# Four batches instead of two take the 32-bit path for the early rows' exponents, and 14 unread products are placed before the second batch's first turn

## The chip, the cores and the metric

The program runs on one core of a Trainium2 chip. The metric is the device time of one execution in microseconds; the figure compared is the median of several executions. A core has a matrix engine (TensorE, PE in the profile, with its weight loads as PEld), a vector engine (VectorE, DVE), an activation engine (ScalarE, ACT), GpSimd (POOL) and SyncE (SP), whose queue issues most of the transfers.

## The reference, cut to what matters

The input has 4 batches of 576 positions and 8 heads of width 64. Three parts follow one another: attention under a mask of blocks of 64, then two feed-forward parts, the second behind a two-dimensional Fourier transform.

```python
scores = scale * np.matmul(q, k.transpose(0, 1, 3, 2))
mask = block_i >= block_j                    # blocks of 64 positions
scores = np.where(mask, scores, -1000000000.0)
scores = scores - np.max(scores, axis=-1, keepdims=True)
attn = np.exp(scores)
attn = attn / (np.sum(attn, axis=-1, keepdims=True) + 1e-09)
attn_out = np.matmul(attn, v)
...
xn = (x - mu) / np.sqrt(var + 1e-06) * g_ln
x = x + np.maximum(xn @ w_ch1, 0.0) @ w_ch2  # 512 -> 2048 -> 512
...
u = x + np.real(np.fft.fft(np.fft.fft(x, axis=1), axis=2))
out = u + np.maximum(norm(u) @ w2_ch1, 0.0) @ w2_ch2
```

## The kernel before

The rows of a batch are cut in three: E is its first 256 positions (the early rows), F another 256, and L holds the 32 or so positions that are left over, of all four batches together. The kernel first computes the attention of the early rows of all batches (E0 to E3), and meanwhile loads the first feed-forward's weights and splits them into a high and a low 16-bit half. As soon as E0 is there, the first feed-forward begins with it (`gemm1`, L632, 8 steps of 24 products per row group; then `gemm2`), and the attention of the remaining rows runs between its products, from `a_switch` on. Everything behind that is the second half and is not touched by the change.

The early rows of a batch are worked off in four pairs of heads, written below as (batch, pair). For each pair: `e_s` computes the scores with 32-bit products (L957) and adds the mask (L917); `e_exp` takes the row maxima on VectorE (L971, L972) and the exponents on ScalarE (L975, four instructions); `e_norm_p` brings the exponents into the transposed layout that the product with V needs; `e_pv` multiplies them with V; `e_x` divides by the row sums on VectorE (L1039, L1042, L1045). There are two ways through the two steps in the middle, and the tuple `ET` says which batches take which:

- The 32-bit way (batches 0 and 1 before the change): `e_turn` transposes the six blocks of 128x128 exponents on TensorE (L986) and ScalarE copies them out of PSUM (L990). `e_pv` first issues `NBUSY` = 4 unread products of 240 columns into the unused part of its PSUM bank (L874), and then six 32-bit products of 65 columns (L1011; each stands as two entries in a trace).
- The 16-bit way (batches 2 and 3): ScalarE and VectorE split the exponents into two halves (`p_split`, L923 and L924), a transposing DMA on SP's queue turns them (`p_turn`, L930), and `e_pv` issues 18 16-bit products (L895). V is scaled and split too (`e_v`, L904 to L908).

V of a 32-bit batch lies in a tile `rv`, of which there are `RVE` = 1 buffers; its four loads (L858) wait for the products of the batch before.

Instructions are written down by `merge`, a planner that interleaves streams by costs, and their order on each engine is then set by a scheduler with priorities. Two things fix a place by hand: `in_order(f)` puts what f issues behind the last TensorE instruction written so far, and `A["busy"]` is a PSUM tile for the unread products in front of batch 0's first turn. Tiles of PSUM for feed-forward products come from `g_tile`, a ring of two buffers, which also gives the tiles `xt` of the normalised rows' turns (`ln_turn`, L587, read by ScalarE at L591 and VectorE at L592).

Of the kernel before, what the change touches and what calls it, by code (L numbers as in the profile page):

```python
# [25 lines left out]
G1P = 20  # L26
G2P = 1
ST = 2
RVE = 1
RAWE = 3  # L30
AP = 20
DW = (3, 5)
# [10 lines left out]
NB = 1  # L43
P_D = 0
EL = 1
ET = (0, 1)
QZ = 3
KB = 3
PSC = 2.0 ** 14
# [6 lines left out]
X0B = 2  # L56
TURN = ((1, ("E", 0)), (1, ("E", 1)))
NBUSY = 4
G1E = 1
LNA = 2  # L60
ESP = 20
# [38 lines left out]
def fused_kernel(ctx: ExitStack, tc: tile.TileContext, io: dict):  # L100
# [14 lines left out]
    def g_tile(shape, name):  # L115


        pool = psg
        if "x" in psn:
            pool = psn["x"] if psn["n"] % (GB + GX) >= GB else psg  # L120
            psn["n"] += 1
        return pool.tile(shape, F32, tag="g", name=name)
# [492 lines left out]
    def gemm1(ffn, c, mp):  # L615
# [21 lines left out]
        h = hT[ffn, c][mp // 2][:, 2 * (mp % 2):2 * (mp % 2) + 2]  # L637
        prio(g1_out, G1E if ffn == 1 and c in (("E", 0), ("E", 1)) else G1P)(ps, h)

# [170 lines left out]
    A = {}  # L810
    ap_ = {}

    def prio(f, n=None):
        def g(*a):
            if (n or AP) <= 0:
                return f(*a)
            with tc.high_priority(n or AP):
                return f(*a)
        return g
# [6 lines left out]
    def a_tile(shape, dt, tag, name):  # L826
        return ap_["p"].tile(shape, dt, tag=tag, bufs=ap_["b"][tag], name=name)
# [25 lines left out]
    def e_load(b):  # L853
        if b in ET:
            r = a_tile([128, NPAIR * 4, 66], F32, "rv", f"rv{b}")
            nc.gpsimd.memset(r[:, :, 64:65], 1.0)
            for p in range(NPAIR):
                (nc.sync if b else nc.scalar).dma_start(  # L858
                    out=r[:, 4 * p:4 * p + 4, 0:64],
                    in_=io["vt"][b, p][:, 0:2, :].rearrange("k c (h d) -> k (c h) d", h=2),  # L860
                )
            A["ev", b] = r
            return
        r = a_tile([128, NPAIR, 256], F32, "rv", f"rv{b}")
        nc.sync.dma_start(
            out=r.rearrange("k p (c d) -> k p c d", c=2),
            in_=io["vt"][b].rearrange("p k c d -> k p c d")[:, :, 0:2, :],
        )
        A["rv", b] = r

    def busy(n, out):

        for _ in range(n):
            nc.tensor.matmul(  # L874
                out=out, lhsT=late[:, 0, :],
                rhs=late.rearrange("p k n -> p (k n)")[:, 0:out.shape[-1]], start=True, stop=True,
            )

    def e_raw(b, p):

        r = a_tile([128, 2, 256], F32, "rz", f"rz{b}{p}")
        nc.sync.dma_start(out=r[:, 0], in_=io["qt"][b, p][:, S:S + 256])
        nc.sync.dma_start(out=r[:, 1], in_=io["kt"][b, p][:, 0:256])
        A["raw", b, p] = r
# [36 lines left out]
    def p_split(e, P, n):  # L921

        nc.scalar.activation(out=P[:, 0, 0:n], in_=e, func=AF.Copy, scale=PSC)  # L923
        nc.vector.scalar_tensor_tensor(  # L924
            out=P[:, 1, 0:n], in0=e, scalar=PSC, in1=P[:, 0, 0:n], op0=ALU.mult, op1=ALU.subtract
        )

    def p_turn(P, blocks):
        PT = a_tile([128, blocks, 128], F16, "PT", "PT")
        nc.sync.dma_start_transpose(out=PT, in_=P.rearrange("p a k -> p (a k)"))  # L930
        return PT
# [13 lines left out]
    def e_s(b, p):  # L945
        with ExitStack() as order:
            if "f" in ff_last:
                order.enter_context(tc.issue_after(ff_last["f"]))
            prio(e_products, ESP)(b, p)
        ff_last["e"] = last_pe()  # L950
# [14 lines left out]
    def e_exp(b, p):  # L965
        st = A.pop(("st", b, p))
        e = a_tile([128, 2, 384], F32, "e", "e")
        q = sm.tile([128, 2, 2, 2], F32, tag="eq", bufs=3, name="eq")
        mx, nb = q[:, 0], q[:, 1]
        for t, (o, w) in enumerate(EO):  # L970
            nc.vector.tensor_reduce(out=mx[:, t], in_=st[:, :, o:o + w], axis=AX.X, op=ALU.max)  # L971
        nc.vector.tensor_scalar(out=nb, in0=mx, scalar1=-0.125, scalar2=None, op0=ALU.mult)  # L972
        for t, (o, w) in enumerate(EO):
            for h in range(2):
                nc.scalar.activation(  # L975
                    out=e[:, h, o:o + w], in_=st[:, h, o:o + w], func=AF.Exp, scale=0.125,
                    bias=nb[:, t, h:h + 1],
                )
        A["e", b, p] = (e, st) if b in ET else e

# [12 lines left out]
    def e_norm_p(b, p):  # L993
        if b in ET:
            return prio(e_turn, ESP)(b, p)
        e = A.pop(("e", b, p))
        P = a_tile([128, 2, 768], F16, "P", "P")
        p_split(e.rearrange("p h k -> p (h k)"), P, 768)
        A["PT", b, p] = p_turn(P, 12)

    @(lambda f: prio(f, EPP))
    def e_pv(b, p):
        if b in ET:
            v, e = A["ev", b], A.pop(("PT", b, p))
            bank = pso.tile([128, 512], F32, tag="o", name="pv")
            busy(NBUSY, bank[:, 272:512])
            ps = bank[:, 0:260].rearrange("q (t h d) -> q t h d", t=2, h=2)
            for t in range(2):
                for h in range(2):
                    for c in range(t + 1):  # L1010
                        nc.tensor.matmul(  # L1011
                            out=ps[:, t, h], lhsT=e[:, h, 128 * (t + c):128 * (t + c) + 128],
                            rhs=v[:, 4 * p + 2 * c + h, 0:65], start=(c == 0), stop=(c == t),
                        )
            A["pv", b, p] = (ps, None)
            return
        vh, vl, s = A["ev", b]
        PT = A.pop(("PT", b, p)).rearrange("k (a h c) q -> k a h c q", a=2, h=2)
        ps = pso.tile([128, 2, 2, 65], F32, tag="o", name="pv")
        for t in range(2):  # L1020
            for h in range(2):
                mm = []
                for c in range(t + 1):
                    n = 4 * p + 2 * c + h
                    for a, v, w in ((0, vh, 65), (0, vl, 64), (1, vh, 65)):
                        mm.append((PT[:, a, h, t + c], v[:, n], w))
                pv(ps[:, t, h], mm)
        A["pv", b, p] = (ps, s)
# [21 lines left out]
    def e_items(b):  # L1050
        def head():
            e_raw(b, 0)
            e_load(b)

        def front(p):
            if p + 1 < NPAIR and b not in ET:
                e_raw(b, p + 1)
            e_s(b, p)
            e_exp(b, p)
            e_norm_p(b, p)  # L1060

        def back(p):
            e_pv(b, p)
            e_x(b, p)

        def two():
            for p in range(2):
                e_s(b, p)
                e_exp(b, p)
            in_order(lambda: (busy(NBUSY, A["busy"][:, 0:384]), e_norm_p(b, 0)) if b == 0 else e_norm_p(b, 0))  # L1070

        if b in ET:
            return [
                (0.0, lambda: [e_raw(b, p) for p in range(3 if b == 0 else 2)], (), None),
                (4.0, lambda: (two(), e_load(b)), (), None),
                (2.0, lambda: (e_raw(b, 2) if b else None, e_norm_p(b, 1)), (), None),
                (3.0, lambda: (e_raw(b, 3), front(2), back(0)), (), None),
                (3.0, lambda: (front(3), back(1)), (), None),
                (1.0, lambda: back(2), (), None),
                (1.0, lambda: back(3), (), ("X1", ("E", b))),  # L1080
            ]

        out = [(0.0, head, (), None), (3.0, lambda: front(0), (), None)]
        out.append((1.0, lambda: e_v(b), (), None))
        for p in range(1, NPAIR):
            out.append((3.0, lambda p=p: (front(p), back(p - EL) if p >= EL else None), (), None))
        for p in range(NPAIR - EL, NPAIR):
            out.append((1.0, lambda p=p: back(p), (), ("X1", ("E", b)) if p == NPAIR - 1 else None))
        return out
# [201 lines left out]
    def last_pe():  # L1291
        return next(
            i for i in reversed(nc.cur_bb.bb.instructions) if i.engine == mybir.EngineType.PE
        )

    def in_order(f):

        with tc.issue_after(last_pe()):
            f()
# [258 lines left out]
    if True:  # L1558
# [31 lines left out]
        ap_["first"] = True  # L1590
        a_open(dict(stage=ST, rv=RVE, rz=RAWE, warm=1, vh=2, vl=2, e=E1B[0], P=E1B[1], PT=E1B[2], xnT0=1, xn0=X0B, unit=1))
        warm = a_tile([128, 1], F32, "warm", "warm")
# [215 lines left out]
```

## Time and profile before

| what | value |
|---|---|
| runs (3) | 980.14, 982.59, 985.02 us; median 982.59 us |
| the profiled execution's own time | 979.0 us |
| its span, first to last instruction | 977.2 us |
| PE busy | 927.8 us, 95% of the span |
| DVE busy | 682.4 us, 70% |
| ACT busy | 491.1 us, 50% |
| mean granted TensorE clock | 0.983 |

The profiled execution is one run of its own, taken by the hardware profiler; it is 3.6 us shorter than the median of the three timed runs. Busy shares are means over stages with different limits, and matmuls are pipelined, so that a busy PE is not PE at its peak.

### The profile page before, as it was taken

The numbers are of one execution on the slowest core, as the hardware profiler recorded it, in microseconds if no ns is written. First come the engines' busy times: TensorE is split into PE (matmuls) and PEld (weight loads), VectorE is DVE, ScalarE is ACT, GpSimd is POOL, SyncE is SP. The second block draws the span as 40 slices with busy tenths as digits, with TensorE's granted clock in tenths as the row PEclk, the third lists the DMA queues.
The fourth block names the chain that finished last, engine by engine and source line by source line (L and its number), as shares of the span: only waits on it lengthen the run. The fifth ranks groups of instructions, "written<-read, shape, count | busy, mean of one in ns | idle before, by whom it ended". The sixth has DMA issues, their size and how long they took to land.

```text
span 977.2 us, 19373 instructions
## 1 busy us (share of the span) xinstructions
PE 927.8 (95%) x7694; PEld 690.0 (71%) x7694; DVE 682.4 (70%) x1716; ACT 491.1 (50%) x860; POOL 73.7 (8%) x183
## 2 busy tenths in 40 slices
PE   8888899997998999999999899999999999999998
PEld 5666644673664765757485767757688888888887
DVE  4887986666667575566599888689486676665754
ACT  5798835554554555437466654335144252352431
POOL 1000000002011020040012201100000000000000
PEclk9798999999999999999999999999999999999999
DMA  8657446667668667577308765102110210101100
GB/s 283 219 201 238 99 122 139 139 130 145 128 141 146 138 139 100 99 188 277 108 22 247 250 217 183 27 11 65 34 22 23 45 22 23 33 24 33 23 23 22
DMA packets 159178, 110.68 MB, mean 113 GB/s; under 512 B 134181, under 2 KB 141350, under 8 KB 157040
## 3 DMA queue, kind: packets, MB, share of 16 engines
q1 hardware_dynamic: 154640, 104.87, 41.6%
q0 software_dynamic: 2336, 4.06, 1.8%
q8 instruction: 60, 0.98, 0.4%
q10 hardware_dynamic: 2112, 0.52, 0.2%
q14 instruction: 30, 0.25, 0.1%
HBM read 63.93 MB, written 11.01 MB: 77 GB/s over the span
## 4 chain that ended last, share of the span: by engine, by line
PE 43%; DVE 7%; DMA 4%; ACT 3%; issue 1%; POOL 0%; SPq 0%; ACTq 0%; DVEq 0%; POOLq 0%
PE g L703 15%; PE s L753 13%; PE g L632 6%; PE g L684 4%; PE g L657 3%; DMA wr<-in_w 2%; DVE wq L345 1%; DVE ws L224 1%; ACT junk L245 1%; DVE hT L642 1%; PE pq L1499 1%; PE ya L1469 1%; DMA d<-ws 1%; ACT sign L223 1%; DMA xnT2('F', 0)_8023<-xs 1%
## 5 line engine op out<-in xcount | busy, mean ns | idle before, releaser
L632 PEld LDWEIGHTS <-wq 128*128 128x128 f16 x2112 | 205.9, 99 | 41.7 <-issue 14.1
L657 PE MATMUL g<-wq,hT 128*128 128x512 f16 x768 | 183.9, 383 | 2.6 <-ACT hT L641 1.6
L703 PEld LDWEIGHTS <-wq 128*128 128x128 f16 x1344 | 131.5, 98 | 15.4
L657 PEld LDWEIGHTS <-hT 128*128 128x128 f16 x768 | 74.6, 99 | 90.4 <-issue 5.5
L753 PEld LDWEIGHTS <-hs 128*128 128x128 f16 x1176 | 115.1, 98 | 13.3
L895 PE MATMUL pv<-vh,PT 128*128 128x65 f16 (+1 forms) x704 | 102.7, 203 | 19.6 <-DMA PT<-P 10.0
L720 ACT ACTIVATE hr<-g,tk 128x256 f32<-128x256 f32 x112 | 47.0, 470 | 143.5 <-PE g L703 143.5
L895 PEld LDWEIGHTS <-PT 128*128 128x128 f16 x1056 | 81.3, 101 | 33.7 <-issue 19.5
L924 DVE SCALAR_TENSOR_TENSOR P<-e,P 128x768 f16<-128x768 f32 (+2 forms) x56 | 54.6, 975 | 68.0 <-ACT P L923 67.9
L728 DVE TENSOR_TENSOR hr<-hr 128x128 f32<-128x128 f32 x224 | 65.4, 292 | 48.3 <-ACT hr L720 40.3
L1177 ACT ACTIVATE e<-st,aq 128x384 f32<-128x384 f32 (+2 forms) x80 | 48.9, 651 | 89.7 <-DVE aq L1174 77.0
L753 PE MATMUL s<-tT,hs 128*128 128x256 f16 x672 | 75.7, 273 | 0.0
L642 DVE SCALAR_TENSOR_TENSOR hT<-g,hT 128x512 f16<-128x512 f32 x88 | 59.7, 682 | 16.4 <-ACT hT L641 16.2
L641 ACT ACTIVATE hT<-g 128x512 f16<-128x512 f32 x88 | 51.3, 584 | 34.9 <-PE g L632 34.8
L684 PE MATMUL g<-wq,hT 128*128 128x512 f16 x288 | 63.9, 379 | 0.0
L895 PE MATMUL pv<-vl,PT 128*128 128x64 f16 (+1 forms) x352 | 62.5, 202 | 0.0
L735 DVE TENSOR_TENSOR hs<-hr,hs 128x896 f16<-128x896 f32 x56 | 60.7, 1084 | 0.5
L753 PE MATMUL s<-tB,hs 128*128 128x256 f16 x504 | 57.3, 273 | 0.0
L223 ACT ACTIVATE sign<-wr 128x512 f16<-128x512 bf16 (+1 forms) x48 | 46.5, 969 | 16.6 <-DMA wr<-in_w 12.9
L734 ACT ACTIVATE hs<-hr 128x896 f16<-128x896 f32 x56 | 53.1, 948 | 1.6 <-DVE hr L728 1.6
L224 DVE SCALAR_TENSOR_TENSOR ws<-wr,sign 128x512 int32<-128x512 int32 (+1 forms) x48 | 41.2, 864 | 17.3 <-ACT sign L223 16.6
L684 PEld LDWEIGHTS <-hT 128*128 128x128 f16 x288 | 28.0, 98 | 31.8
(432 smaller groups left out, 1504.7 us busy)
## 6 DMA issues: line engine op xcount, KB each, us to landing
wr<-in_w SPq DMA_DIRECT2D x16, 1023.5 KB, 6.2
wr<-in_w SPq DMA_DIRECT2D x32, 511.8 KB, 4.7
rawv<-in_vt SPq DMA_DIRECT2D x16, 320.0 KB, 3.2
k<-in_kt SPq DMA_DIRECT2D x16, 288.0 KB, 3.4
d<-ws SPq DMA_DIRECT2D x4, 1024.0 KB, 4.8
ws<-d SPq DMA_DIRECT2D x4, 1024.0 KB, 5.2
wt<-d SPq DMA_DIRECT2D x4, 1024.0 KB, 4.8
qz<-in_qt SPq DMA_DIRECT2D x32, 80.0 KB, 3.2
```

What stands on the lines that cost most here:

```text
L223: nc.scalar.activation(out=z[:, :, :, 1], in_=r.bitcast(BF16)[:, :, :, 2], func=AF.Copy)
L632: nc.tensor.matmul(out=ps[:, i, :], lhsT=w1(ffn, k, wh, m), rhs=xt[:, xh, k, :], start=(n == 0), stop=(n == 3 * KT - 1),)
L642: nc.vector.scalar_tensor_tensor(out=h[:, :, 1, :], in0=ps, scalar=0.0, in1=h[:, :, 0, :], op0=ALU.max, op1=ALU.subtract,)
L657: nc.tensor.matmul(out=ps, lhsT=h[f // 4][:, f % 4, hh, t * 128:(t + 1) * 128], rhs=w2(ffn, f, wh), start=(f == 0 and hh == 0 and wh == 0) ...
L684: nc.tensor.matmul(out=g2["b"][t], lhsT=h[f // 4][:, f % 4, hh, t * 128:(t + 1) * 128], rhs=w2(ffn, f, wh), start=(f == 0 and hh == 0 and ...
L703: nc.tensor.matmul(out=ps[:, q, :], lhsT=w1(2, k, wh, i + 8 * q), rhs=xt[:, xh, k, :], start=(n == 0), stop=(n == 3 * KT - 1),)
L728: done = nc.vector.tensor_tensor(out=r[:, o], in0=r[:, a], in1=r[:, b], op=op)
L734: nc.scalar.activation(out=h[:, 0], in_=r[:, 1:8], func=AF.Copy)
L735: nc.vector.tensor_tensor(out=h[:, 1], in0=r[:, 1:8], in1=h[:, 0], op=ALU.subtract)
L753: nc.tensor.matmul(out=ps, lhsT=h[:, hh, hb], rhs=T[nm][:, wh, i], start=(i == 0 and hh == 0 and wh == 0), stop=(i == 7 and hh == 1),)
L895: nc.tensor.matmul(out=out[..., 0:w], lhsT=l, rhs=v[..., 0:w], start=(n == 0), stop=(n == len(mm) - 1))
L924: nc.vector.scalar_tensor_tensor(out=P[:, 1, 0:n], in0=e, scalar=PSC, in1=P[:, 0, 0:n], op0=ALU.mult, op1=ALU.subtract)
```

## The change

Batches 2 and 3 move to the 32-bit way (`ET`), `rv` gets a second buffer (`RVE`), and 14 unread products of 384 columns are issued ahead of batch 1's first turn, into a new tile from the ring of `g_tile`. Below `e_items`, batches 2 and 3 now take the list of items of the 32-bit branch: two pairs' scores and exponents first, V's loads then, and a later start of the products with V.

```diff
-RVE = 1
+RVE = 2
...
-ET = (0, 1)
+ET = (0, 1, 2, 3)
...
+NBUSY1 = 14
...
-            in_order(lambda: (busy(NBUSY, A["busy"][:, 0:384]), e_norm_p(b, 0)) if b == 0 else e_norm_p(b, 0))
+            if b == 0:
+                in_order(lambda: busy(NBUSY, A["busy"][:, 0:384]))
+            elif b == 1:
+                in_order(lambda: busy(NBUSY1, g_tile([128, 512], "busy")[:, 0:384]))
+            in_order(lambda: e_norm_p(b, 0))
```

The scheduler's order moves with it. On TensorE, in front of E0's first feed-forward product, the kernel before has these rows (e_379 and e_397 are the exponents of pairs (1,0) and (1,1), xn0 are E0's normalised rows, rv1 is batch 1's V; a bracket names what the instruction waits for).

```order
L874 MATMUL pv_612<-late_83 128x240
L986 MATMUL st_370<-unit_117,e_379 128x128 [waits DVE_49,Activation_49]
L1011 MATMUL pv_520<-rv1_414,PT_412 128x65 [waits DMAHW6_49,Activation_49,Pool_49]
L986 MATMUL st_388<-unit_117,e_397 128x128 [waits DVE_49,Activation_49]
L874 MATMUL pv_663<-late_83 128x240 [waits PE_49]
L587 MATMUL xt_332<-unit_117,xn0_330 128x128 [waits DVE_49]
L587 MATMUL xt_341<-unit_117,xn0_339 128x128 [waits DVE_49]
L1011 MATMUL pv_612<-rv1_414,PT_453 128x65 [waits DMAHW7_49,Activation_49]
L632 MATMUL g1_464<-xnT0_329,wq110_360 128x256 [waits Activation_49]
```

With the change the same place reads as follows (all lines of the file move down by one; busy_406 is the new tile of the unread products).

```order
L875 MATMUL pv_627<-late_83 128x240
L987 MATMUL st_388<-unit_117,e_397 128x128 [waits DVE_49,Activation_49]
L588 MATMUL xt_332<-unit_117,xn0_330 128x128 [waits DVE_49]
L588 MATMUL xt_341<-unit_117,xn0_339 128x128 [waits DVE_49]
L875 MATMUL busy_406<-late_83 128x384 [waits DVE_49]
L987 MATMUL st_370<-unit_117,e_379 128x128 x6
L633 MATMUL g1_479<-xnT0_329,wq110_360 128x256 [waits DVE_49]
```

The turn of pair (1,1) now stands first, then E0's turns, then the 14 products, which wait for VectorE, then the turn of (1,0); both pairs' products with V (L1011) have moved behind E0's first feed-forward step.

On VectorE, in the chain of small steps that normalises E0, the kernel before has a pair's division in the middle, which waits for TensorE.

```order
L224 SCALAR_TENSOR_TENSOR ws_422<-wr_356,sign_119 128x1024
L552 TENSOR_TENSOR ln1('E', 0)_310<-ln1('E', 0)_310 128x2
L1039 TENSOR_SCALAR rr<-pv 128x4
L553 SCALAR_TENSOR_TENSOR ln1('E', 0)_310<-ln1('E', 0)_310 128x2
L1042 RECIPROCAL rr<-rr 128x4
```

With the change the chain stands there alone.

```order
L225 SCALAR_TENSOR_TENSOR ws_437<-wr_356,sign_119 128x1024
L553 TENSOR_TENSOR ln1('E', 0)_310<-ln1('E', 0)_310 128x2
L554 SCALAR_TENSOR_TENSOR ln1('E', 0)_310<-ln1('E', 0)_310 128x2
```

The division of (1,0) has moved behind the feed-forward's first step.

On TensorE, in batch 3, the kernel before places 18 products of 16 bits per pair between feed-forward products (here at pair (3,1); the last two rows repeat with the other blocks).

```order
L684 MATMUL g_1581<-wq_1544,hT 128x512
L895 LDWEIGHTS PT
L895 MATMUL pv<-vh_1385,PT 128x65
L895 LDWEIGHTS PT
L895 MATMUL pv<-vl_1386,PT 128x64
```

With the change each pair of batches 2 and 3 has a turn, placed inside a feed-forward step, and later four unread products and six products of 32 bits.

```order
L685 MATMUL g_1575<-wq_1497,hT 128x512
L987 MATMUL st<-unit,e 128x128 x6
L685 LDWEIGHTS hT
...
L685 MATMUL g_1576<-wq_1497,hT 128x512
L875 LDWEIGHTS late
L875 MATMUL pv<-late 128x240
...
L1012 MATMUL pv<-rv_1351,PT 128x65 x6
```

From the feed-forward's `gemm2` of E0 on, behind the last early pair, TensorE's order is the same in both kernels.

## Rows read from the trace of the kernel before

**Rows 1.** Busy time by stretch: from:to, length, engines (instructions), granted clock, DMA share, GB/s

```profile
core 0: us, PE busy (x) PEld busy (x) DVE busy (x) ACT busy (x) POOL busy (x), PEclk, DMA share, GB/s
30.24:44.54 14.30, 9.98 (x50) 8.70 (x50) 10.99 (x38) 9.92 (x18) 0.38 (x1) 0.64 0.70 218
44.54:78.85 34.31, 30.25 (x251) 24.00 (x250) 29.88 (x80) 30.02 (x44) 1.77 (x4) 0.95 0.55 189
78.85:97.47 18.62, 14.77 (x142) 11.87 (x138) 13.75 (x34) 15.45 (x27) 1.51 (x3) 0.91 0.98 304
97.47:146.06 48.59, 44.15 (x403) 27.79 (x403) 42.08 (x109) 29.90 (x48) 1.98 (x11) 1.00 0.49 109
```

**Rows 2.** PE's waits from 44.5 to 146 us: total, times, longest

```profile
PE pv L895 <- DMA PT<-P: 8.3, 6, 3.8
...
PE st L986 <- ACT e L975: 0.8, 2, 0.4
```

**Rows 3.** Instructions in time order before the first feed-forward: start, length, engine, line

```profile
33.04 1.54 PE L986 MATMUL st<-unit,e 128*128 128x128 f32 x6 [2.79 <-ACT e L975]
...
33.56 0.37 ACT L975 ACTIVATE e<-st,eq 128x128 f32<-128x128 f32 x1 [0.58 <-DVE eq L972]
...
38.35 0.16 DVE L1039 TENSOR_SCALAR rr<-pv 128x4 f32<-128x4 f32 x1 [2.96 <-PE pv L1011]
...
40.08 1.00 DVE L570 TENSOR_SCALAR xn<-XxE,ln1('E', 0)_310 128x512 f32<-128x512 f32 x2
...
40.68 1.97 PE L587 MATMUL xt<-unit,xn 128*128 128x128 f32 x8 [0.28 <-DVE xn L570]
...
43.21 1.28 DVE L592 TENSOR_TENSOR xnT<-xt,xnT 128x512 f16<-128x512 f32 x2
...
44.54 2.67 PE L632 MATMUL g<-xnT,wq 128*128 128x256 f16 x23 [0.31 <-DVE xnT L592]
```

**Rows 4.** Busy time of two stretches, columns as in rows 1

```profile
33.04:42.44 9.40, 8.17 (x36) 7.15 (x37) 6.09 (x26) 6.71 (x10) 0.38 (x1) 0.50 0.73 259
...
94.57:97.03 2.46, 2.46 (x26) 2.00 (x27) 1.19 (x4) 0.84 (x3) 0.00 (x0) 0.50 1.07 386
```

**Rows 5.** PE's 32-bit and unread products in time order, 2 to 60 us

```profile
2.51 1.76 PE L874 MATMUL busy<-late 128*128 128x384 bf16 x5
...
56.10 1.45 PE L1011 MATMUL pv<-rv,PT 128*128 128x65 f32 x12
...
57.39 0.57 PE L874 MATMUL pv<-late 128*128 128x240 bf16 x4
...
57.80 0.71 PE L632 MATMUL g<-xnT,wq 128*128 128x256 f16 x5
...
58.94 0.88 PE L986 MATMUL st<-unit,e 128*128 128x128 f32 x6 [0.44 <-ACT e L975]
...
59.66 1.04 PE L632 MATMUL g<-xnT,wq 128*128 128x256 f16 x8
```

**Rows 6.** One 16-bit pair in batch 2, PE alone, in time order

```profile
104.36 0.20 PE L895 MATMUL pv<-vh,PT 128*128 128x65 f16 x1 [1.21 <-DMA PT<-P]
...
104.92 1.25 PE L632 MATMUL g<-xnT1('E', 1)_848,wq 128*128 128x256 f16 x10
```

**Rows 7.** Around E1's turns, in time order

```profile
71.10 0.63 PE L587 MATMUL xt<-unit,xn 128*128 128x128 f32 x4 [1.79 <-DVE xn L570]
...
73.33 4.60 PE L632 MATMUL g<-xnT,wq 128*128 128x256 f16 x24 [0.60 <-DVE xnT1('E', 1)_848 L592]
```

**Rows 8.** Groups by line from 60 to 146 us: busy, mean ns, idle before

```profile
L924 DVE SCALAR_TENSOR_TENSOR P<-e,P 128x768 f16<-128x768 f32 x8 | 7.6, 949 | 0.0
...
L908 DVE SCALAR_TENSOR_TENSOR vl<-rv,pw,vh 128x1024 f16<-128x1024 f32 x2 | 2.6, 1277 | 0.0
```

**Rows 9.** The last early pair and the first score of the later attention

```profile
137.00 0.20 PE L895 MATMUL pv<-vh,PT 128*128 128x65 f16 x1 [1.01 <-DMA PT<-P]
...
146.06 0.92 PE L1153 MATMUL st<-k,qz 64*128 64x384 f32 x4
```

## Prediction

> **What bounds the kernel now.** I read the busy times by stretch first, to find where TensorE still has room. In the stretch up to the first feed-forward product it is busy 9.98 of 14.30 us at a granted clock of 0.64; from there to 78.85 us 30.25 of 34.31; then 14.77 of 18.62; and from 97.47 to 146.06 us, where batches 2 and 3 are mostly worked off, 44.15 of 48.59 [rows 1]. In the last of these ScalarE (29.90) has much room and VectorE (42.08) little more than TensorE. So TensorE is the engine to add work to last, and what can be won is its idle time and its half clock.
>
> The view of TensorE's waits says what that idle time is: 8.3 us in six waits for the transposing DMA, the longest 3.8; the exponents of a 32-bit pair cost it 0.8 us in two waits [rows 2]. The instructions in time order show the front: before 33.04 us TensorE has waited 2.79 us for the exponents of (1,0), and from there the clock stays at 0.50, that is 1.2 of 2.4 GHz, until 42.44 us although the engine is busy 8.17 of 9.40 us, with 32-bit turns, sums and a few unread products [rows 3, 4]. After the 3.8 us wait it is 0.50 again for 2.46 us [rows 4].
>
> From the attention's first score at 146.06 us on TensorE's order doesn't change. I take the time there as the handle: whatever that instruction is late or early, the end is too.
>
> **The change part by part.** The sum stands against the profiled execution's own 979.0 us.
>
> *A, the start of the first feed-forward (44.54 us before [rows 3]).* The order shows that the 14 products don't cover the wait for the second batch's exponents: the turn of (1,1) and E0's own turns stand ahead of them, and they wait for VectorE, because their tile is the ring buffer that E0's first turns leave. Walked through: TensorE is idle from 30.25 us (33.04 less 2.79) until the exponents of (1,1). Their first instruction starts at 33.56; without the copy of (1,0) between them, four of 0.37 at most end by 35.0. The turn at half clock takes 1.54: 36.5. VectorE's chain for E0 no longer waits 2.96 us for the pair's sum, nor does its division; so the normalised rows, at 40.08 to 41.08 before, come some 3.5 us earlier, 36.6 to 37.6. The eight turns of 1.97 us end by about 39.3; copy and subtraction (the latter 1.28 for both) free the first buffer near 41.0. Then the 14 products: five of this size took 1.76 us at the kernel's start, so 14 take 4.9; at full clock, from four of 240 columns in 0.41 us (57.39 to 57.80), 0.164 each, 2.3 [rows 3, 5]. I take 3.8, as the clock has been low since the wait and should rise on the way: 44.8. The turn of (1,0) costs 0.72 (58.94 to 59.66 [rows 5]): 45.5. **+1.0**, bounds -3.0 (everything at full clock and no wait for VectorE) and +3.0 (half clock into the first feed-forward step, whose 24 products take 4.60 us where 23 took 2.67 [rows 3, 7]).
>
> *B, displaced work.* The sums of (1,0) and (1,1) and four unread products stood in that stretch and now stand behind the feed-forward's start. A sum of six products costs 1.29 us (56.10 to 57.39), four unread ones 0.41 [rows 5]: 2 x 1.29 + 0.41 = **+3.0**.
>
> *C, E1's turns.* TensorE waits 1.79 us for E1's normalised rows, and 0.60 more for a buffer [rows 7]. This chain hangs on the sum of (1,3), behind which TensorE now has about eight tenths more work before the turns (two more groups of four unread products); so **-0.8**; bounds -2.4 (both waits gone) and +3.0 (a decoding step of VectorE now stands between E1's normalised rows and the subtraction that frees the buffer, and E0's later weights go through the same engines).
>
> *D, eight pairs change their way.* Each gains a turn (0.72), a sum (1.29) and four unread products (0.41), 2.42 us, and loses 18 16-bit products, 0.56 us (104.36 to 104.92 [rows 6]). Net 1.86, times eight **+14.9**. If a turn costs its whole 0.88 us of record, it is +16.2. These lie between feed-forward products that follow each other without a gap, so nothing hides them.
>
> *E, the waits for the transposing DMA* go: 8.3 us [rows 2], and half of the 2.46 us at half clock behind the longest, 1.2 [rows 4]: **-9.5**. No reason for less: the transfer itself is gone.
>
> *F, new waits.* Each turn waits for its pair's exponents. Two such waits cost 0.4 each before [rows 2]; eight of them 0 to 3.2; the scheduler places a turn 14 to 23 products into a step, which covers most: **+1.5**.
>
> *G, what costs nothing.* VectorE loses eight splits of exponents (7.6 us) and two of V (2.6) [rows 8], ScalarE trades each split for a copy of the same size: both are beside TensorE's work, and what their lightening can give is in C and F. SP's queue loses eight transposes and gets V earlier; the loads for the later attention still wait for the last early pair, which before ended some 8.5 us ahead of the first score (137.00, 146.06 [rows 9]) and after has more feed-forward products behind it; if that cover were gone, the load's few us would show there.
>
> Sum: 1.0 + 3.0 - 0.8 + 14.9 - 9.5 + 1.5 = **+10.1 us**, 989.1 us of own time. The median of the runs before is 982.6, 3.6 above the profiled execution; a median after is then about 992.7, and I say **992 us**.
>
> A rule speaks to D. A 32-bit sum has twelve entries in 1.29 us, 108 ns each, the 16-bit one 18 in 0.56, 31 ns each [rows 5, 6]. The Trainium skill (TensorE: Matmul & The Clock Gate, "Weight-path perf modes — Fast Weight Load (FWL) and DoubleRow") says that the fast weight load is on for 128 weights of any type but FP32, and measures its gain at about two times. By that an entry would cost 62 ns, a sum 0.75, D 4.3 us less and B 1.1 less: +4.7 us. The rows' factor is 3.5, and they have the 32-bit sum itself; I go by them.
>
> **The rivals.**
> - *No change (within 0.5%, that is 4.9 us, about what a measurement of this kernel can tell).* The gaps of the front are all filled: A at -3.0, C at -2.4, F at 0: -3.0 + 3.0 - 2.4 + 14.9 - 9.5 = +3.0, 985.6. For it: VectorE's chain no longer waits for TensorE. Against it: the products stand behind a buffer that VectorE frees.
> - *Faster, because the early stages are paced by VectorE and not by TensorE.* VectorE is busy 29.88 of 34.31 and 42.08 of 48.59 us [rows 1], and the change takes 10.2 us from it [rows 8]. If that set the pace, the time would fall by up to that, to 972. It decides only if TensorE has room for what it gets (B and D, 17.9 us) and for the shortening: 28 us of idle time between 44.54 and 146.06. Rows 1 give 4.06 + 3.85 + 4.44 = 12.4 us, so I hold it for unlikely.
> - *Slower still, by the clock.* All upper bounds: 3.0 + 3.0 + 3.0 + 16.2 - 9.5 + 3.2 = +18.9, 1001.5. For it: 32-bit turns and sums ran for 9.40 us without lifting the clock [rows 4], and the change puts only such work ahead of the 14 products. Against it: from 44.54 us on turns stand inside steps of dense products. To this row: the Trainium skill (TensorE: Matmul & The Clock Gate, "Part 4: PE-mode transpose") says that transposes don't count as busy for the clock in the same way; the trace agrees for the front, and no row shows it for a turn inside a step.
> - *The change doesn't do what it says.* By the order the 14 products are not ahead of the turn that TensorE meets first; this is already in A.
>
> **How the numbers follow.** Forecast (slower by 5 to 15 us) 0.62; the clock rival (over 15) 0.13; no change 0.18; faster 0.07. Slower is the first two, 0.75. The range leaves out the faster rival and the ends of the others: from 984 (just below the all-filled case) to 1001 (the clock rival's sum), 8 in 10 or a little more. The likeliest case alone has 988 to 997.
>
> **What would show it.** Right: the attention's first score near 156 us instead of 146.06; no wait for the transposing DMA before it; the turn of (1,1) starting near 35 us behind an idle TensorE, and the 14 products behind E0's turns with a wait for VectorE; in batches 2 and 3 a TensorE without gaps, with 2.4 us for each pair. Wrong: the first feed-forward product before 42 us (A); E1's turns without any wait in front and a clock of 1.00 behind them (C); turns waiting a us or more each (F); or the shift at the first score being given back later, by a wait of the attention that hangs on something other than TensorE.

## The result: 1% slower

The kernel with the change has a median of 992.43 us (985.69 to 995.64, 20 runs), the kernel before, on the same chip, 981.69 (978.11 to 989.94, 20 runs). The ratio is 1.0095, with a 95% interval of 1.0074 to 1.0117: +9.3 us, 7.3 to 11.5. Its profiled execution has a span of 990.8 us, where the span of before was 977.2.

All file lines are one higher than before, and five higher for the later attention. TensorE in time order at the front, as in [rows 3]:

```profile
30.90 0.58 PE L875 MATMUL pv<-late 128*128 128x240 bf16 x4 [0.28 <-DVE XxE L1046]
36.21 1.54 PE L987 MATMUL st<-unit,e 128*128 128x128 f32 x6 [4.72 <-ACT e L976]
38.64 2.00 PE L588 MATMUL xt<-unit,xn 128*128 128x128 f32 x8 [0.89 <-DVE xn L571]
42.28 4.25 PE L875 MATMUL busy<-late 128*128 128x384 bf16 x14 [1.64 <-DVE xnT L593]
46.37 0.82 PE L987 MATMUL st<-unit,e 128*128 128x128 f32 x6
47.02 2.79 PE L633 MATMUL g<-xnT,wq 128*128 128x256 f16 x24
...
76.00 0.63 PE L588 MATMUL xt<-unit,xn 128*128 128x128 f32 x4 [1.48 <-DVE xn L571]
76.96 0.66 PE L588 MATMUL xt<-unit,xn 128*128 128x128 f32 x4 [0.34 <-DVE hT L643]
78.69 2.78 PE L633 MATMUL g<-xnT,wq 128*128 128x256 f16 x24 [1.08 <-DVE xnT1('E', 1)_863 L593]
...
107.64 0.57 PE L875 MATMUL pv<-late 128*128 128x240 bf16 x4
108.05 1.46 PE L1012 MATMUL pv<-rv,PT 128*128 128x65 f32 x12
109.35 0.57 PE L875 MATMUL pv<-late 128*128 128x240 bf16 x4
...
157.45 0.92 PE L1158 MATMUL st<-k,qz 64*128 64x384 f32 x4
```

The wait for the exponents has grown from 2.79 to 4.72 us, the 14 products stand behind E0's turns and another wait of 1.64, and the first feed-forward starts at 47.02. Below, E1's turns still wait, but the 24 products behind them take 2.78 us where [rows 7] have 4.60. The first score of the later attention has moved from 146.06 [rows 9] to 157.45.

Busy time by stretch, columns as in [rows 1]:

```profile
30.90:47.02 16.12, 8.87 (x38) 5.62 (x39) 14.98 (x40) 10.74 (x18) 0.59 (x1) 0.68 0.63 210
47.02:78.69 31.67, 28.14 (x254) 24.33 (x252) 25.63 (x71) 26.94 (x40) 1.61 (x4) 1.00 0.58 182
78.69:100.00 21.31, 18.92 (x175) 15.74 (x174) 13.64 (x32) 17.04 (x28) 0.77 (x2) 1.00 0.65 235
100.00:157.45 57.45, 56.32 (x426) 40.04 (x426) 38.60 (x113) 30.68 (x55) 2.57 (x13) 1.00 0.24 66
```

In the last stretch TensorE is busy 56.32 of 57.45 us, at full clock: the idle time of before is gone, and what is left is work. VectorE (38.60) is no bound there. TensorE's waits from 44.5 to 157 us:

```profile
PE st L987 <- ACT e L976: 3.9, 7, 1.9
PE xt L588 <- DVE xn L571: 1.5, 1, 1.5
PE g L633 <- DVE xnT1('E', 1)_863 L593: 1.1, 1, 1.1
PE xt L588 <- DVE hT L643: 0.3, 1, 0.3
```

No wait for the transposing DMA is left (8.3 us in [rows 2]); the turns' waits for exponents are 3.9 us where two of them cost 0.8.

### The profile page after: what moved, and what is told of

Its sections match the earlier page's. It is cut to its first block, busy times and chain, and to the rows that moved or that the text cites. A ratio compares the mean times of both kernels' runs of the same rounds, so it can differ in the third digit from the quotient of the medians.

```text
span 990.8 us, 19432 instructions
## 1 busy us (share of the span) xinstructions
PE 941.7 (95%) x7740; PEld 702.6 (71%) x7740; DVE 674.0 (68%) x1698; ACT 486.9 (49%) x854; POOL 72.2 (7%) x181
## 4 chain that ended last, share of the span: by engine, by line
PE 43%; DVE 7%; DMA 4%; ACT 3%; issue 1%; POOL 0%; SPq 0%; ACTq 0%; POOLq 0%; DVEq 0%
PE g L704 15%; PE s L754 13%; PE g L633 6%; PE g L685 4%; PE g L658 3%; DMA wr<-in_w 3%; DVE wq L346 1%; ACT junk L246 1%; DVE ws L225 1%; ACT sign L224 1%; PE pq L1504 1%; DVE hT L643 1%; PE ya L1474 1%; DMA xnT2('F', 0)_7978<-xs 1%; ACT junk L1389 0%
## 5 line engine op out<-in xcount | busy, mean ns | idle before, releaser
L896 PE MATMUL pv<-vh,PT 128*128 128x65 f16 (+1 forms) x608 | 95.7, 202 | 11.2 <-DVE aq L1179 5.4
L925 DVE SCALAR_TENSOR_TENSOR P<-e,P 128x768 f16<-128x768 f32 (+2 forms) x48 | 47.1, 980 | 70.1 <-ACT P L924 70.0
L896 PEld LDWEIGHTS <-PT 128*128 128x128 f16 x912 | 75.4, 100 | 22.9 <-issue 18.0
L896 PE MATMUL pv<-vl,PT 128*128 128x64 f16 (+1 forms) x304 | 56.6, 202 | 0.0
L224 ACT ACTIVATE sign<-wr 128x512 f16<-128x512 bf16 (+1 forms) x48 | 46.5, 971 | 13.6 <-DMA wr<-in_w 11.8
```

What stands on the lines that cost most here:

```text
L224: nc.scalar.activation(out=z[:, :, :, 1], in_=r.bitcast(BF16)[:, :, :, 2], func=AF.Copy)
L896: nc.tensor.matmul(out=out[..., 0:w], lhsT=l, rhs=v[..., 0:w], start=(n == 0), stop=(n == len(mm) - 1))
```

## The experiments

Two theories stood at the start. *P*: the eight pairs' 32-bit work makes the loss. *Fr*: the front makes it, the new order and the 14 products in front of the first feed-forward. Each kernel has 6 to 12 runs (after 20), compared with runs of the kernel before on the same chip. One table for all: what the profile of each says of the stage that differs ("E0 ends" and "E1" are the end of E0's first feed-forward step and start and end of E1's, 24 products each; "score" is the first score of the later attention), and the whole time against before, by the ratio and its interval on 982 us (the ratio takes in all runs and can differ by a us or two from the medians').

| kernel | E0 ends | E1 | score | median | against before, us |
|---|---|---|---|---|---|
| before | 47.21 | 73.33–77.93 | 146.06 | | |
| after | 49.81 | 78.69–81.47 | 157.45 | 992.43 | +9.3 (7.3 to 11.5) |
| f1_front | 49.32 | 78.55–83.38 | 153.79 | 988.37 | +5.8 (3.7 to 7.9) |
| f2_rv | 48.25 | 75.63–80.27 | 150.24 | 982.25 | +0.3 (-2.0 to 2.7) |
| f3_pairs | 48.05 | 74.16–78.33 | 154.98 | 985.85 | +3.6 (1.2 to 6.2) |
| f4_no4 | 49.70 | 78.60–83.88 | 156.62 | 992.17 | +9.2 (5.9 to 12.7) |
| f5_some | 49.86 | 78.73–81.51 | 155.63 | 990.34 | +8.6 (5.6 to 11.8) |
| i3_two | 48.21 | 77.16–82.01 | 149.60 | 982.13 | +0.7 (-2.0 to 3.3) |
| h1_bank | 43.39 | 72.72–77.57 | 143.88 | 982.82 | +0.8 (-1.8 to 3.4) |
| h4_bank_all | 43.77 | 74.98–79.24 | 155.94 | 986.21 | +6.0 (3.4 to 8.4) |
| g1_lag | 48.40 | 74.51–78.69 | 152.13 | 983.51 | +2.2 (-0.1 to 4.3) |
| i1_fill | 44.00 | 74.94–79.28 | 149.35 | 981.01 | -1.4 (-4.2 to 1.4) |
| i2_fill_all | 43.39 | 72.80–75.58 | 152.66 | 987.02 | +3.4 (1.0 to 5.9) |
| j1_fill20 | 44.13 | 73.48–76.26 | 146.39 | 981.77 | -1.3 (-3.5 to 1.0) |

A caution on the columns: they are one execution each. The profiled one of before took 979.0 us, 2.7 under its median, that of f2_rv 985.91, 3.7 over its median, that of j1_fill20 975.12, 6.65 under. f2_rv has nearly TensorE's order of before and comes to the first score 4.2 us later; and the way from the first score to the end of the span, which no edit touches, takes 826.6 (h4_bank_all) to 837.2 us (h1_bank). Part of that scatter is the clock: summed over stretches of 2 us by their granted clock, the time at half clock on this way is 10 us in each of the two shortest (h4_bank_all, j1_fill20) and 20 and 27 us in the two longest (h1_bank, f5_some). So the whole times decide, and the columns say where.

**f1_front: the front alone** (against after; batches 2 and 3 by the 16-bit way).

```diff
-ET = (0, 1, 2, 3)
+ET = (0, 1)
```

> Batches 2 and 3 stay on the 16-bit way; the 14 unread products and the second buffer of V are in. The front of TensorE's order is then that of the change. Theory P (the eight pairs' 32-bit work makes the loss): only the front's part is left. In the changed kernel's trace the products of E0 behind E1's turns end 3.5 us later than before, so about +3.5 us against before. Theory Fr (the front makes the loss): +8 us or more, near the changed kernel.

Measured: +5.8 us, more than half of the loss, though no pair of batches 2 and 3 has changed its way. That lies between the numbers of the two theories (+3.5, and +8 or more).

**f2_rv: only the second buffer for V** (against before).

```diff
-RVE = 1
+RVE = 2
```

> The kernel before with only the second buffer of V's 32-bit tile. Both theories: no change (0 +- 1.5 us), since V's loads are early enough; if SP's queue, which no longer waits for the first batch's sums, is worth something, 1 to 2 us faster; if weights come later by the loads that now stand ahead of them, the 1.2 us by which the changed kernel's front is late at 30 us shows here.

Measured: +0.3, nothing. With it, what f1_front loses is down to the 14 products and the order that they bring.

**f3_pairs: the pairs alone** (against after).

```diff
-            elif b == 1:
-                in_order(lambda: busy(NBUSY1, g_tile([128, 512], "busy")[:, 0:384]))
```

> All four batches on the 32-bit way, second buffer of V, but without the 14 unread products; the front of TensorE's order is then that of before. Theory P: 14.9 us of added work less 9.5 of waits plus some 3 of new waits, about +8 us against before. Theory Fr: 0 to +2 us.

Measured: +3.6, again between the two. The halves add up, 5.8 + 3.6 = 9.4 to after's 9.3: neither theory alone, both.

**f4_no4: after without the four unread products of each pair of batches 2 and 3.**

```diff
-            busy(NBUSY, bank[:, 272:512])
+            busy(NBUSY if b < 2 else 0, bank[:, 272:512])
```

> The changed kernel without the four unread products ahead of each of the eight pairs' sums of batches 2 and 3 (32 products of 240 columns left out, whose results nobody reads). Theory P with dense work: 8 x 0.41 = 3.3 us faster than the changed kernel, +7 to +8 against before. Rival, the clock: these products keep it at full speed among 32-bit work; without them stretches at half clock appear after 80 us and the time is that of the changed kernel or more.

Measured: +9.2, as after, with 32 products fewer. TensorE in time order at E1's turns says where their time went, and the stretch of E1's first step says at which clock:

```profile
75.90 0.63 PE L588 MATMUL xt<-unit,xn 128*128 128x128 f32 x4 [1.92 <-DVE xn L571]
...
78.60 5.28 PE L633 MATMUL g<-xnT,wq 128*128 128x256 f16 x24 [1.08 <-DVE xnT1('E', 1)_863 L593]
```

```profile
78.60:83.80 5.20, 5.20 (x24) 3.34 (x23) 2.35 (x7) 2.80 (x3) 0.38 (x1) 0.50 0.91 305
```

In after eight of these products (the first two pairs of batch 2) stand ahead of E1's turns, and the step behind them takes 2.78 us at a granted clock of 1.00; here it takes 5.28 at 0.50. The eight themselves save nothing here, since the turns start at the same time (76.00 in after) and wait 1.92 instead of 1.48 us; the 2.5 us lost at the step are what the other 24 (0.10 each) can give. Over all runs the mean granted clock is 0.983 here and 0.985 in after.

**f5_some: those eight kept, the other 24 left out** (against after).

```diff
-            busy(NBUSY, bank[:, 272:512])
+            busy(NBUSY if (b, p) < (2, 2) else 0, bank[:, 272:512])
```

> The kernel after with the four unread products a pair of batches 2 and 3 kept only for the first two pairs of batch 2, which stand ahead of the second batch's first-layer turns, and left out for the other six pairs (24 products fewer). If f4_no4 lost at these turns, through the half clock, what it won by leaving out the products: the turns' feed-forward at full clock (2.8 us for its first 24 products, not 5.3), and the whole time 2 to 3.5 us below the kernel after, +6 to +8 us against before. If the unread products are needed all along the pairs: within 1 us of the kernel after, +9 to +11 us.

Measured: E1's step at full clock again, 2.78 us, as the clock story of f4_no4 expects; and from its end to the first score 74.12 us where after has 75.98, 1.9 less, of the 2.5 that 24 products cost. The whole time, +8.6, can't show it: its interval holds after's +9.3, and the expected +6 to +8 too. Nor do all runs together: their mean granted clock, 0.983, is that of f4_no4.

**i3_two: f1_front with 2 of the 14 products** (against f1_front).

```diff
-NBUSY1 = 14
+NBUSY1 = 2
```

> f1_front with 2 of the 14 unread products instead of 14: the same order of the turns in front of the first feed-forward, in the same ring of buffers, without the products' own 4.25 us. If the products' own time made the front dear: first feed-forward 3 to 4 us earlier than in f1_front (42.5 to 43.5 us), whole time +1 to +3 us against before. If the new order of the turns made it dear (the turn of pair (1,1) first, a wait of 4.7 us), or the clock, which stays at half without the products: first feed-forward above 44.5 us or its first 24 products in more than 4 us, whole time +4 to +6 us.

Measured: +0.7, so f1_front's loss is gone, with the new order of the turns and its wait of 4.72 us still there. TensorE in time order:

```profile
35.69 1.54 PE L987 MATMUL st<-unit,e 128*128 128x128 f32 x6 [4.72 <-ACT e L976]
...
41.76 0.80 PE L875 MATMUL busy<-late 128*128 128x384 bf16 x2 [1.64 <-DVE xnT L593]
42.35 1.48 PE L987 MATMUL st<-unit,e 128*128 128x128 f32 x6
43.63 4.58 PE L633 MATMUL g<-xnT,wq 128*128 128x256 f16 x24
```

The first step starts at 43.63 and runs at half speed, 4.58 us, as the rival says, and the whole time is still the lower one. The 14 products raise the clock at this step and cost more than that gives: with them the step is done at 49.32, without 48.21. By the whole times twelve of them cost 5.8 - 0.7 = 5.1 us (1.7 to 8.5, from the two intervals). The two profiles are 1.1 us apart at the end of E0's step, 1.4 at the end of E1's and 4.2 at the first score, the last within the scatter of single profiles; where a difference of 5 us would arise isn't settled. The clock as a whole isn't higher with 14 than with 2: its mean over the runs is 0.980 in both.

**h1_bank: the products in front of the wait** (against f1_front).

```diff
-                in_order(lambda: busy(NBUSY1, g_tile([128, 512], "busy")[:, 0:384]))
+                in_order(lambda: busy(NBUSY1, pso.tile([128, 512], F32, tag="o", name="busy")[:, 0:384]))
```

> The kernel before (first two pairs in 32 bits, the other six in 16 bits, unread products of batch 2 by two), with the 14 unread products of 512 columns written into a PSUM bank of the attention's accumulators instead of the ring of the scores, so that they stand directly behind the first scores of the layer, ahead of the turn that TensorE waits for first; the seven unread products of 240 columns follow them. Theory W (in the kernel after, the 14 products were in the wrong place: behind the turns, where no wait was left to fill; in front of the first wait they keep TensorE at full clock and cost no time of their own): first feed-forward at 43 to 44.5 us instead of 44.5 to 45.0, granted clock near 1.00 from about 38 us on, whole time -2 to -5 us against before. Rival A (unread products cost their own time wherever they stand, or VectorE sets the front): first feed-forward at 45 to 47, whole time 0 to +3 us.

The expectation misnames three things: the products have 384 columns, the tile left is the ring of the feed-forward's products, and it is the first two batches that take the 32-bit way. A bank of the accumulators needn't wait for E0's turns, so the products come first, and the sums of (1,0) and (1,1) stand ahead of the first feed-forward again, as in before. TensorE in time order, and two stretches:

```profile
29.12 2.45 PE L875 MATMUL busy<-late 128*128 128x384 bf16 x14
...
32.84 0.88 PE L987 MATMUL st<-unit,e 128*128 128x128 f32 x6 [0.55 <-ACT e L976]
...
40.61 2.78 PE L633 MATMUL g<-xnT,wq 128*128 128x256 f16 x24
...
69.77 1.58 PE L588 MATMUL xt<-unit,xn 128*128 128x128 f32 x8 [3.30 <-DVE xn L571]
72.72 4.85 PE L633 MATMUL g<-xnT,wq 128*128 128x256 f16 x24 [1.37 <-DVE xnT1('E', 1)_863 L593]
```

```profile
32.84:40.61 7.77, 5.90 (x50) 5.35 (x50) 6.74 (x27) 6.60 (x11) 0.53 (x1) 1.00 0.56 179
...
60.02:72.72 12.70, 6.83 (x55) 5.60 (x54) 12.15 (x36) 12.70 (x18) 1.68 (x3) 0.90 0.61 205
```

The front does what theory W says: the products fill the wait (0.55 us is left of it), the clock stays at 1.00 through the turns and sums, which ran at 0.50 in [rows 4], and the feed-forward starts at 40.61, 3.9 us before [rows 3]. The whole time doesn't follow: +0.8, where W has -2 to -5. Of the 3.9 us, 1.3 are left at E1's turns and 0.4 at the end of E1's step (77.57 against 77.93), since the turns, which waited 1.79 us for E1's normalised rows in [rows 7], now wait 3.30. VectorE in time order, the first step of that normalisation and the rows, here:

```profile
60.49 0.69 DVE L536 BATCH_NORM_STATS2 bn1('E', 1)0_845<-XxE 128x6 f32<-128x512 f32 x1
...
69.09 1.00 DVE L571 TENSOR_SCALAR xn<-XxE,ln1('E', 1)_844 128x512 f32<-128x512 f32 x2
```

And in the kernel before:

```profile
63.18 0.69 DVE L535 BATCH_NORM_STATS2 bn1('E', 1)0_830<-XxE 128x6 f32<-128x512 f32 x1
...
70.41 1.00 DVE L570 TENSOR_SCALAR xn<-XxE,ln1('E', 1)_829 128x512 f32<-128x512 f32 x2
```

The chain starts 2.7 us earlier and ends 1.3 earlier: two more steps of the feed-forward (0.68 and 0.75 us) stand between its links. From 60.02 to 72.72 us VectorE is busy 12.15 of 12.70 us and ScalarE, which also decodes weights, all of them. So the wait that bounds next stood there already, with 1.79 us. The first score is 2.2 us earlier than in before; that the whole time shows nothing of it isn't settled, as the rest of the span, here the longest of all, scatters by more.

**h4_bank_all: the same place, all eight pairs** (against after, the same two lines).

> The kernel after (all eight pairs in 32 bits), with the 14 unread products written into the accumulators' bank as in h1_bank, so that they stand ahead of the first turn. If front and pairs add up, as their single runs did (+5.8 us for the front alone, +3.6 us for the pairs alone), and the place of the products is what made the front dear: before -1 to +3 us, that is 7 to 10 us quicker than the kernel after. If the products cost their own time wherever they stand: +7 to +10 us against before, like the kernel after.

Measured: +6.0, between the two: E0's step ends 6 us earlier than in after (43.77), as h1_bank's does against f1_front, the whole time comes 3.3 us below after's, and E1's turns wait 3.63 us here too, with 4.26 us for the step behind them.

**g1_lag: 16-bit pairs one pair later**, with a third buffer for the turned exponents (against before).

```diff
-E1B = (3, 2, 2)
+E1B = (3, 2, 3)
...
-EL = 1
+EL = 2
```

> The kernel before with the products of its 16-bit pairs one pair later, so that each transposing transfer has one more pair's work to hide behind. The kernel before waited 8.3 us in this stage for those transfers, and the kernel after took those waits away but won less than that. If those waits were time that could be won (as the prediction's sum has it): whole time -2 to -5 us against before. If they only stood where another wait, on VectorE's or ScalarE's work, would stand instead: -1 to +1 us.

Measured: no gain (+2.2, -0.1 to 4.3). TensorE's waits in this kernel from 27 to 150 us:

```profile
PE pv L895 <- DMA PT<-P: 9.1, 5, 4.2
PE st L986 <- ACT e L975: 3.5, 3, 2.8
```

9.1 us for the transposing DMA where before had 8.3: one pair more of cover made the waits no shorter here, though other kernels with the same transfers have 5.1 (h1_bank) and 7.8 us (j1_fill20). So this run doesn't tell what the waits are worth.

**i1_fill, i2_fill_all: products ahead of E1's turns too** (against h1_bank and h4_bank_all, in `ln_turn`).

```diff
+        fill = (ffn, c, t) == (1, ("E", 1), 0) and pso.tile([128, 512], F32, tag="o", name="busy")
...
+            if fill is not False:
+                busy(NBUSY1, fill[:, 0:384])
```

> h1_bank with 14 more unread products of 384 columns directly ahead of E1's turns, in a bank of the accumulators, where h1_bank waited 3.30 us for VectorE's normalised rows and then ran its next 24 products in 4.85 us. Theory (the front's 4 us went into this wait, since VectorE works without a gap from 60 us until E1's rows are there; what is left to win is the clock behind it): E1's turns no earlier than in h1_bank (69 to 70.5 us), the next 24 products in 2.8 us at full clock, first score some 2 us earlier, whole time 1 to 3 us below h1_bank, -2 to +1 us against before. Rival (the products go on the path as they do in the kernel after): E1's turns 2.3 us later, whole time +1 to +3 us against before.

> h4_bank_all with the same 14 unread products ahead of E1's turns. Theory: E1's turns at the same time (72.5 us), the next 24 products in 2.8 us instead of 4.26, whole time 0 to 2 us below h4_bank_all, +2 to +4.5 us against before, so that what is left is the price of the eight pairs. Rival: the products go on the path, +5 to +8 us.

Measured: i1_fill -1.4, i2_fill_all +3.4. In i2_fill_all the fill did what it should; TensorE in time order:

```profile
66.32 2.44 PE L878 MATMUL busy<-late 128*128 128x384 bf16 x14
68.59 0.98 PE L878 MATMUL pv<-late 128*128 128x240 bf16 x8
70.42 1.11 PE L591 MATMUL xt<-unit,xn 128*128 128x128 f32 x8 [0.84 <-DVE xn L571]
72.80 2.78 PE L636 MATMUL g<-xnT,wq 128*128 128x256 f16 x24 [1.26 <-DVE xnT1('E', 1)_863 L596]
```

22 products lie in the wait, the turns are no later than in h4_bank_all (72.48), and the step is at full clock. All eight pairs in 32 bits then cost +3.4 instead of +9.3, and the mean granted clock over the runs rises from 0.988 in h4_bank_all to 0.992. In i1_fill 14 products left 1.05 us of the wait, and the step took 4.34 us: its expectation failed in that. Its turns came at 71.99, 2.2 us after h1_bank's, as the rival has it; but the products end before the rows are there, and 2.0 of the 2.2 us lie ahead of them (E0's step ends 0.6 later, and a step at 51.48 takes 4.14 us where h1_bank's takes 2.79).

**j1_fill20: 20 products there** (against i1_fill, `NBUSY1 + 6`).

> i1_fill with 20 unread products ahead of E1's turns instead of 14: six more take 1.0 us, and i1_fill still waited 1.05 us there and ran the next 24 products in 4.34 us. If the clock behind E1's turns hangs on the idle time that is left around them (i2_fill_all, with 14 products of 384 columns and 8 of 240, kept full clock with waits of 0.84 and 1.26 us): the wait for the rows under 0.3 us, the next 24 products in 2.8 us, whole time -2 to -4 us against before. If it doesn't: 4.3 us again for the 24 products, whole time within 1 us of i1_fill, -2 to +1 us against before.

Measured: the wait 0.15 us, the step 2.78 us, as expected; the whole time -1.3 (-3.5 to 1.0), not the -2 to -4 but what the other answer expects. The profile is the fastest of the twelve runs, at a mean clock of 0.993; six of the twelve have 0.983 or 0.984, like i1_fill's profile, so the full clock at this step isn't shown for the usual run. TensorE waits 7.8 us for the transposing DMA in this kernel, and the granted clock from 81 to 100 us is 0.91. No kernel tried is faster than the one before beyond its interval; i1_fill and j1_fill20 are at its level.

## Why the prediction was right

992 us was forecast and 992.43 measured, and the reason is the one given: TensorE gets more work than it had idle time. That it fits to half a us is luck: the change is known as +9.3 (7.3 to 11.5), and the 3.6 us added to the sum for the median of three runs are 2.7 by twenty. In the two profiles the shift can be followed through the terms. Before anything changes, after is already 1.24 us late (its wait begins at 36.21 - 4.72 = 31.49; before's at 33.04 - 2.79 = 30.25); this is scatter and not V's second buffer, since g1_lag, with one buffer, is as late. So of the 11.39 us at the first score 10.15 are the change's; the sum was +10.1.

- *A (predicted +1.0).* Less the 1.24, the walk holds row by row: the turn of (1,1) at 34.97 (35.0), the normalised rows, which start at 38.04 on VectorE, at 36.8 (36.6), the 14 products at 41.04 (41.0) for 4.25 us (3.8). The first feed-forward is 47.02 - 44.54 - 1.24 = +1.2.
- *B and C (+3.0 and -0.8).* At the end of E1's first step after is 81.47 - 77.93 - 1.24 = 2.3 us late where A + B + C give 3.2. C had the wrong reason: the two waits around E1's turns, 1.48 and 1.08 us, are together no shorter than 1.79 and 0.60 [rows 7]; what fell is the step, 4.60 to 2.78, by the clock, on which the prediction had nothing here, although it had the 4.60 in its rows. Without these 1.8 us, as in f1_front, whose step takes 4.83, the front costs +4.4 at this point (83.38 - 77.93, less the 1.0 by which its wait begins later).
- *D + E + F (+6.9).* From that point to the first score: 75.98 against 68.13, +7.85. The seven kernels with two 32-bit batches and one pair's lag take 66.3 to 70.4 (mean 68.9), the four with eight more pairs and all their unread products 76.0 to 77.1 (76.6): +7.7. A sum takes 1.30 us and four unread products 0.41 (108.05 to 109.35, 107.64 to 108.05), as D has them. F was too small: the turns' waits rose by 3.1 us, not 1.5, at the upper bound given.
- *G (nothing).* From the first score to the end: 831.1 us before and 833.35 after, inside the scatter of 826.6 to 837.2. So the first score is a handle on the end only to that scatter.

The whole times divide it otherwise. The front alone is +5.8 (f1_front) where A + B + C have 3.2. The pairs cost 3.6 (f3_pairs), 3.5 (f1_front to after), 5.2 (h1_bank to h4_bank_all) and 4.8 us (i1_fill to i2_fill_all) where D + E + F have 6.9. So the direction and the mechanism are as forecast, but the good sum is in part luck, two errors of opposite sign. What the pairs' sum leaves out is the clock: in all four comparisons the eight pairs raise its mean over the runs (0.983 to 0.987, 0.980 to 0.985, 0.986 to 0.988, 0.986 to 0.992). An estimate from this: 0.0025 to 0.005 of 980 us are 2 to 5 us, if TensorE works all through these stretches; the pairs are 1.7 to 3.4 us cheaper than the sum. Where this clock is won is shown for one place in single profiles only, E1's step, with the pairs' eight unread products ahead of it.

The rivals: "no change" asked for filled gaps in the front; h1_bank shows that filling them alone gains nothing against before, with VectorE's chain to E1's turns as the next wait; i2_fill_all, with that wait filled too, comes to +3.4, near this rival's +3.0. "VectorE paces the stages" is true of that one place and not of the pairs, where TensorE is busy 56.32 of 57.45 us. "By the clock" went the other way: 1.00 from 47.02 to 157.45 us.

On term D the rows were right to go by: the Trainium skill (TensorE: Matmul & The Clock Gate, "Weight-path perf modes — Fast Weight Load (FWL) and DoubleRow") measures the fast load, which FP32 does not get, at about two times; after's sums, twelve entries in 1.30 us, are 108 ns an entry again, 3.5 times the 31 ns of [rows 6]. An entry's time covers the product and its weight load together, so no run here tests the page's factor by itself.

## What to carry to other kernels

Unread products that keep TensorE's clock up were free inside a wait that is there anyway: ahead of the wait they filled it (h1_bank, +0.8); behind it 12 more of them cost some 5 us (1.7 to 8.5, f1_front against i3_two). Look in the order at which buffer they get, since that decides where they stand. And a way that is quicker for an idle TensorE (a turn on the engine in place of a transfer) is slower where the engine is nearly full: count its idle time in that stage before adding to it. If a bound is taken away, ask which engine's chain stands next: here E1's turns already waited 1.79 us for VectorE.

## What the hardware showed beside this

The granted clock at one place isn't set by the order alone. In g1_lag the waits around E1's turns are those of [rows 7] (1.80 and 0.60 us), with the same instructions in front, and TensorE in time order shows the step behind them at full clock:

```profile
72.29 0.63 PE L587 MATMUL xt<-unit,xn 128*128 128x128 f32 x4 [1.80 <-DVE xn L570]
73.25 0.66 PE L587 MATMUL xt<-unit,xn 128*128 128x128 f32 x4 [0.34 <-DVE hT L642]
74.51 1.19 PE L632 MATMUL g<-xnT,wq 128*128 128x256 f16 x8 [0.60 <-DVE xnT1('E', 1)_848 L592]
76.43 0.50 PE L632 MATMUL g<-xnT,wq 128*128 128x256 f16 x3 [0.73 <-DVE wq L345]
77.10 1.59 PE L632 MATMUL g<-xnT,wq 128*128 128x256 f16 x13 [0.16 <-DVE wq L345]
```

Of the seven kernels with unread products directly ahead of these turns, five kept full clock (after, f3_pairs, f5_some, i2_fill_all, j1_fill20); of the seven without, this one. That suggests that the products make it likelier; with one profile a kernel it isn't shown, and a single pair such as f4_no4 and after doesn't prove it. Nor is all of the clock's gain kept: at full speed the step here waits 0.73 and 0.16 us for weights that VectorE is still decoding, which at half clock were there in time. What a kept clock is worth can be seen inside j1_fill20, one program: its four runs at a mean clock of 0.991 or more take 975.1 to 979.7 us, its other eight, at 0.983 to 0.988, 978.1 to 984.0.
